# Laying out the transposed Q/K buffer by head: one buffer and one scratch format of a gated attention and feed-forward kernel

## The chip, the core and the metric

The kernel runs on one core of one Trainium2 chip. The metric is the device time of one execution in microseconds (us), as the median over several executions. The profile comes from one further execution, whose own time is given beside its span.

## What is computed

Two branches run over the same 2048 rows of 1024 values and are mixed by a sigmoid gate. Branch B is a feed-forward net of width 3584. Branch A is attention with a recurrent memory: the rows are cut into 64 segments of 32, each segment sees 8 memory rows ahead of it, and the first 8 rows of its output are the memory of the next segment. So the segments of branch A run strictly one after the other.

```python
def _A_ref(x, mem0, Wq, Wk, Wv, Wo, seg_len):       # 32 heads of 128, M = 8, seg_len = 32
    mem = mem0
    for s in range(n_seg):                          # 64 segments
        xs = x[:, s * seg_len:(s + 1) * seg_len, :].copy()
        h = jnp.concatenate([mem, xs], axis=1)      # 40 rows
        q = jnp.einsum('btd,dhe->bhte', h, Wq)
        k = jnp.einsum('btd,dhe->bhte', h, Wk)
        v = jnp.einsum('btd,dhe->bhte', h, Wv)
        scores = jnp.einsum('bhqe,bhke->bhqk', q, k) * scale
        scores = jnp.where(mask[None, None], scores, -1000000000.0)
        p = _softmax(scores, axis=-1)
        o = jnp.einsum('bhqk,bhke->bhqe', p, v)
        o = jnp.einsum('bhte,hed->btd', o, Wo)
        mem = o[:, :M, :].copy()
        outs.append(o[:, M:, :])
...
g = _sigmoid((x * gate_w).sum(-1, keepdims=True))
return g * a + (1 - g) * b                          # b = (gelu(x @ w_gate) * (x @ w_up)) @ w_down
```

All inputs and weights are bf16.

## The kernel before

**Stages.** Branch B comes first (to about 600 us of the span). Then the 64 segments of branch A follow, some 24.8 us each. The weights of branch A do not all fit on the chip: most lie in the buffers `arena`, `low`, `extra` and so on; 14 pieces of 512 KB per segment are read again each time into `ring`, a ring of 8 slots of which one piece takes two. SyncE's queue issues such a load (line 693) when the matmuls that used the slots before are done, so that up to four are under way.

**Rows of a segment.** A segment's 40 rows are split. Its 8 memory rows and the last 24 of its own rows (together 32, in `hT`) are projected when the segment runs (`emit_P`, line 1087). The first 8 rows of every segment ("ext" rows in the code) do not depend on the memory; they are projected earlier for four segments at once (`emit_ext`, line 897, 4 x 8 rows in `xe`), in rounds that a hand-written list puts between the other matmuls (token `F`). When such a projection is complete, `end_rows` takes it from the bank `pbc` to `rowsx`. For Q and K it is then transposed (`go`, line 1010), taken from PSUM back into the same `rowsx` by four VectorE copies, one for each of the four segments (`put`, line 1023), and written by a GpSimd DMA to the DRAM scratch `qk_scr` (line 1026). `load_ext` reads a segment's part of it into `pn` one segment ahead (line 795).

**Q and K of a segment.** The work is done in two halves `h` of 16 heads. A projection puts its 32 rows four times beside each other: partitions 32g to 32g+31 of a bank hold the rows for the four heads i = 0..3 of group g. The bank goes to `rows`, and `emit_T` (matmuls of line 1133, copy of line 920 or 922) transposes it, so that a PSUM bank holds, for each of the 128 dimensions of a head, values in the order (i, g, row). The copy moves these to the buffer `qk`, and `emit_qke` (line 1152 on ScalarE for the half 0, line 1154 on VectorE for the half 1) puts the 8 ext rows of each head behind them. In each segment `emit_T` runs four times, with its copy twice on VectorE and twice on ScalarE.

**Scores.** `emit_S` (line 1171) then forms the 40 x 40 scores of 16 heads with 16 matmuls. Two heads run beside each other, one with its result on partitions 0 to 39, one on 64 to 103; each has its own Q as stationary operand (40 columns) and its own K as moving operand (40 columns). The softmax follows (VectorE lines 1178 to 1189, ScalarE's exponential in line 1184, VectorE line 1194), then its transposition (`emit_PT`, line 1204), the product with V (`emit_PV`, line 1231) and the output projection (`emit_O`, line 1279). At the end of a segment `mem` and `mem_T` (line 1345, copies in lines 1352 and 1355) bring the new memory into `hT`.

**The order.** Nothing reorders at run time. `PLAN` is a list of tokens by hand, the same for all segments but the first, that says in which order the operations are put into the engines' queues; every engine runs its own in that order and waits on semaphores. `F` carries four numbers, one for each place of a segment in a group of four: so many waiting rounds of the ext projections or the ext rows' output are put there. These pieces of it matter here:

```python
("T", 1, "dve", 32, 4), ("P", "q", 1, 2), ("F", (1, 1, 0, 0)), ("P", "q", 1, 2), ("F", (10, 0, 0, 6)), ("flush", 128, 4),
("S", 0), ("P", "k", 1, 2), ...
("PV", 0, 4, "act", "act"), ("S", 1), ("F", (1, 1, 5, 0)), ("O", 0, 2), ...
("M", 1, "act"), ("MT", 1), ("F", (0, 1, 1, 0)), ("OB", 1), ("bh", 0, "act"), ("M", 0, "dve"), ("F", (0, 0, 1, 1)), ("flush", 128, 3)
```

`flush` is `go` and `put` of a finished ext projection. `put_out` (line 1358, VectorE) comes early in the next segment: it reads a finished segment's output from its bank `pba` or `pbb`, which the projections of the next segment use again.

Between its uses for scores `qk` also holds a piece of a weight (`flat_qk`, written as flat memory by line 1067 and read by lines 1087 and 897).

Of the kernel before, what the change touches and what calls it, by code (L numbers as in the profile page):

```python
# [5 lines left out]
BF16 = mybir.dt.bfloat16  # L6
# [122 lines left out]
def bass_gated_mix__memory_aug_recurrent_mem_tr__geglu_ffn__prompt_kernel(  # L129
# [21 lines left out]
    SEG = 32  # L151
    L = SEG + M
# [11 lines left out]
    EXT = 8  # L164
    GR = 4
    QK_RES, V_RES, O_RES = 6, 6, 4

    with ExitStack() as es:
# [23 lines left out]
        def SB(shape, dt, name):  # L192
            return es.enter_context(nc.sbuf_tensor(name, list(shape), dt))
# [3 lines left out]
        xe = nc.alloc_sbuf_tensor_at("xe", [128, KC, SEG], BF16, offset=LOW + 14336)  # L197
        rows = SB([128, 512], BF16, "rows")
        rowsx = SB([128, 512], BF16, "rowsx")
        qk = SB([128, 2, 4, L, 4], BF16, "qk")  # L200
        vt = SB([128, 2, 512], BF16, "vt")
        pn = SB([128, 8, 80], BF16, "pn")
        pnf = pn[:, :, :].rearrange("p a b -> p (a b)")
# [1 line left out]
        qkst = [pnf[:, 256 * h:256 * (h + 1)] for h in range(2)]  # L205
# [20 lines left out]
        PBV = [p[:, :].bitcast(BF16) for p in PB]  # L226
# [4 lines left out]
        g = _Sched()  # L231
# [16 lines left out]
        def A(c):  # L248
# [6 lines left out]
           r=[("ident",)], w=[("ident",)])  # L255
# [67 lines left out]
        for side in range(2):  # L323
            op("pool", lambda e, side=side: e.memset(bm[64 * side:64 * side + L, side:side + 1], 1.0),
               r=[("bm",)], w=[("bm",)])
# [312 lines left out]
        for tok, *arg in PLAN:  # L638
            if tok in ("P", "O", "OA"):
# [3 lines left out]
                for x in range(x0, x0 + n):  # L643
                    k = KORD[who][x] if tok == "P" else OORD[who[1]][x]
                    u = (*who, k - k % 2 if tok != "P" and (*who, k) not in wide else k)
# [272 lines left out]
        def copy(eng, dst, src, r, w):  # L918
            if eng == "act":
                op("act", lambda e: e.activation(dst, src, ACTF.Copy), r=r, w=w)  # L920
            else:
                op("dve", lambda e: e.tensor_copy(dst, src), r=r, w=w)
# [48 lines left out]
        for s in range(NSEG):  # L971
# [18 lines left out]
            def end_rows(m, h, j):  # L990
                if s == 0:
                    rx, kx, sx = stage(m, h)
                else:
                    flush()
                    rx, kx, sx = rowsx[:, :], RX, "rowsx"
                op("act", lambda e: e.activation(rx, PB[B_X][:, :], ACTF.Copy), r=[P(B_X)], w=kx)  # L996
                if m == "v":
                    def put():
                        op("pool", lambda e: e.dma_start(v_scr[j, h, :, :, :, :].rearrange("g u r c -> (g u r) c"), rx),
                           r=kx, w=[("vscr", j, h)], dsem="%sv" % sx)  # L1000
                    vput.append(put) if s == 0 else put()
                    return
                mi = "qk".index(m)

                def go(w=32, bank=B_T):
                    def mk(e):
                        ins = None
                        for i in range(4):
                            for y in range(0, 128, w):
                                ins = e.transpose(PBV[bank][y:y + w, i * 128:(i + 1) * 128],  # L1010
                                                  rx[:, i * 128 + y:i * 128 + y + w], ident[:, :])
                        return ins
                    op("pe", mk, r=[*kx, ("ident",)], w=[P(bank)])
                    return bank

                def put(bank):
                    st = rx.rearrange("p (u g r i) -> p u g r i", u=GR, g=4, r=EXT)
                    src = PBV[bank][:, 0:512].rearrange("p (i g u r) -> p u g r i", i=4, g=4, u=GR)

                    def cp(e):  # L1020
                        ins = None
                        for u in range(GR):
                            ins = e.tensor_copy(st[:, u], src[:, u])
                        return ins
                    op("dve", cp, r=[P(bank)], w=kx)
                    op("pool", lambda e: e.dma_start(  # L1026
                        qk_scr[j * GR:(j + 1) * GR, :, h, mi, :].rearrange("u p x -> p u x"),
                        rx.rearrange("p (u x) -> p u x", u=GR)),
                       r=kx, w=[("qkscr", j, h, mi)], dsem=sx)
                post.append((go, put))  # L1030


# [95 lines left out]
            def emit_T(m, eng="dve", w=32, bank=B_T):  # L1128
                def mk(e):
                    ins = None  # L1130
                    for i in range(4):
                        for j in range(0, 128, w):
                            ins = e.transpose(PBV[bank][j:j + w, i * 128:(i + 1) * 128],  # L1133
                                              rows[:, i * 128 + j:i * 128 + j + w], ident[:, :])
                    return ins
                op("pe", mk, r=[("rows",), ("ident",)], w=[P(bank)])
                copy(eng, qk[:, m, :, 0:SEG, :], PBV[bank][:, 0:512].rearrange("p (i g c) -> p g c i", i=4, g=4),
                     [P(bank)], [("qk", m)])

            def emit_qke(h, eng="dve", s=s, ms=(0, 1)):  # L1140
                if s == 0:
                    for mi in ms:
                        m = "qk"[mi]
                        rx, kx, _ = stage(m, h)
                        src = rx[:, 0:128].rearrange("p (g x) -> p g x", g=4)
                        op("dve", lambda e, mi=mi, src=src: e.tensor_copy(
                            qk[:, mi, :, SEG:L, :].rearrange("p g c i -> p g (c i)"), src), r=kx, w=[("qke",)])
                    return
                dst = qk[:, :, :, SEG:L, :].rearrange("p m g c i -> p m g (c i)")
                src = qkst[h].rearrange("p (m g x) -> p m g x", m=2, g=4)  # L1150
                if eng == "act":
                    op("act", lambda e: e.activation(dst, src, ACTF.Copy), r=[("qkst", h)], w=[("qke",)])
                else:
                    op("dve", lambda e: e.tensor_copy(dst, src), r=[("qkst", h)], w=[("qke",)])
# [9 lines left out]
            def emit_S(h, s=s):  # L1164
                def mk(e):
                    ins = None
                    for x in range(8):
                        for side in range(2):
                            p0 = SIDES[side]
                            gq = 2 * (x // 4) + side  # L1170
                            ins = e.matmul(PB[B_S][p0:p0 + L, x * L:(x + 1) * L],  # L1171
                                           lhsT=qk[:, 0, gq, :, x % 4], rhs=qk[:, 1, gq, :, x % 4], start=True, stop=True,
                                           skip_group_check=True)
                    return ins
                op("pe", mk, r=[("qk", 0), ("qk", 1), ("qke",)], w=[P(B_S)])
                sv = PB[B_S][0:104, 0:8 * L].rearrange("p (i c) -> p i c", i=8)
                mxv = mx[0:104, :]
                op("dve", lambda e: e.scalar_tensor_tensor(  # L1178
                    out=sv, in0=sv, scalar=scale, in1=mask[0:104, None, :].to_broadcast([104, 8, L]),
                    op0=ALU.mult, op1=ALU.add), r=[("mask",)], w=[P(B_S)])  # L1180
                op("dve", lambda e: e.tensor_reduce(mxv, sv, AX.X, ALU.max), r=[P(B_S)], w=[("mx",)])
                op("dve", lambda e: e.tensor_tensor(out=sv, in0=sv, in1=mxv[:, :, None].to_broadcast([104, 8, L]),  # L1182
                                                    op=ALU.subtract), r=[("mx",)], w=[P(B_S)])
                op("act", lambda e: e.activation(sv, sv, ACTF.Exp), w=[P(B_S)])  # L1184
                if s and h == 0:
                    emit_qke(1)
                op("dve", lambda e: e.tensor_reduce(mxv, sv, AX.X, ALU.add), r=[P(B_S)], w=[("mx",)])  # L1187
                op("dve", lambda e: e.reciprocal(mxv, mxv), w=[("mx",)])
                op("dve", lambda e: e.tensor_tensor(  # L1189
                    out=rr[0:104, :, :], in0=mx[0:104, :, None].to_broadcast([104, 8, 2]),  # L1190
                    in1=bm[0:104, None, :].to_broadcast([104, 8, 2]), op=ALU.mult), r=[("mx",), ("bm",)], w=[("rr",)])
                gates = [("z", t) for t in range(NT)] + [("th", t) for t in range(NT)] if s == 0 and h == 0 else []
                for c0, k0, n in ((0, 0, SEG), (2 * SEG, SEG, EXT)):
                    op("dve", lambda e, c0=c0, k0=k0, n=n: e.tensor_tensor(  # L1194
                        out=pn[0:104, :, c0:c0 + 2 * n].rearrange("p i (two c) -> p i two c", two=2),
                        in0=sv[:, :, None, k0:k0 + n].to_broadcast([104, 8, 2, n]),
                        in1=rr[0:104, :, :, None].to_broadcast([104, 8, 2, n]), op=ALU.mult),
                       r=[P(B_S), ("rr",)], w=[("pn", c0), ("qkst", 0), ("qkst", 1)] + PTB + gates)
# [363 lines left out]
```

## Time and profile before

| | |
|---|---|
| device time, median of 3 executions | 2206.41 us (2202.46 to 2207.2) |
| the profiled execution: device time | 2207.77 us |
| the profiled execution: span from the first to the last instruction | 2205.9 us |
| mean granted TensorE clock in it | 0.994 |
| VectorE, ScalarE, GpSimd busy | 52%, 42%, 21% of the span |
| read from and written to HBM | 596.71 MB and 34.59 MB |

In the profile PE is TensorE's matmuls, PEld its loads of the stationary operand (they overlap matmuls), DVE is VectorE, ACT ScalarE, POOL GpSimd and SP SyncE; a q behind an engine's name is its DMA queue. A group of the profile is written as line, engine, operation, output and input; the banks of PSUM are `pba` to `pbh`. A matmul's recorded duration is the time until its last result stands, most of which is the way through the array; matmuls that follow each other overlap, so what a block of them costs is seen from start to start.

### The profile page before, as it was taken

The page shows a single profiled execution, that of the slowest core. Times are in us where ns is not written, and L with a number is a line of the kernel's source. Part 1 is how long each engine was busy: PE and PEld are TensorE (multiplying, and loading weights), DVE is VectorE, ACT ScalarE, POOL GpSimd, SP SyncE. Part 2 cuts the span into 40 slices and gives each one's busy share as a digit, 9 for nine tenths or more (in the row PEclk, how much of TensorE's full clock was granted, in tenths as well). Part 3 has the DMA queues.
Part 4 walks back from the last instruction along what each step waited for, and adds up shares of the span by engine and source line. Part 5 has one row for each costly group of instructions (what it writes and reads, how often), then busy time and mean ns, then how long its engine had stood idle before and what let it go on. Part 6 is the DMA issues. An engine that isn't in the chain of part 4 may idle for free.

```text
span 2205.9 us, 78545 instructions
## 1 busy us (share of the span) xinstructions
PE 2104.6 (95%) x35368; PEld 1107.8 (50%) x35424; DVE 1154.8 (52%) x2680; ACT 935.6 (42%) x1960; POOL 461.6 (21%) x814
## 2 busy tenths in 40 slices
PE   9999999999998999999999999999999999999987
PEld 4444444444454555555454545555455555555544
DVE  5716536345054555555555555555555555555554
ACT  4403324133044444544454445444444444444443
POOL 1020020140122222222122222222122222222221
PEclk9999999999999999999999999999999999999999
DMA  8726625346888999999999999999999999999997
GB/s 271 276 70 220 215 58 194 122 148 202 302 302 301 325 326 328 326 338 328 330 317 327 325 319 329 323 324 320 315 323 328 332 330 329 337 333 323 324 325 245
DMA packets 247377, 629.21 MB, mean 285 GB/s; under 512 B 37393, under 2 KB 106081, under 8 KB 246273
## 3 DMA queue, kind: packets, MB, share of 16 engines
q1 hardware_dynamic: 215732, 573.14, 74.5%
q0 software_dynamic: 30112, 50.48, 7.4%
q8 instruction: 278, 4.55, 0.8%
q10 hardware_dynamic: 1196, 0.56, 0.1%
q14 instruction: 59, 0.48, 0.1%
HBM read 596.71 MB, written 34.59 MB: 286 GB/s over the span
## 4 chain that ended last, share of the span: by engine, by line
PE 77%; DMA 15%; DVE 4%; ACT 2%; issue 2%; POOL 0%; SPq 0%; DVEq 0%; POOLq 0%; ACTq 0%
PE pba L1087 13%; PE pbb L1087 12%; DMA ring<-w_scr 11%; PE pbc L897 6%; PE pbb L1279 4%; DMA hT<-xT_scr 3%; PE pba L1279 3%; PE pbc L1258 3%; PE pba L466 2%; PE pbh L466 2%; PE pbg L466 2%; PE pbf L466 2%; PE pbe L466 2%; PE pbb L466 2%; PE pbd L466 2%; PE pbc L466 2%
## 5 line engine op out<-in xcount | busy, mean ns | idle before, releaser
L1087 PE MATMUL pba<-arena,hT 128*32 128x512 bf16 x4416 | 357.1, 383 | 5.1 <-DVE bo L1358 4.4
L1087 PE MATMUL pbb<-arena,hT 128*32 128x512 bf16 x4416 | 355.6, 383 | 1.3 <-issue 1.3
L897 PE MATMUL pbc<-arena,xe 128*32 128x512 bf16 x2208 | 190.0, 381 | 3.4 <-ACT rowsx L996 2.0
L803 POOL DMA_DIRECT2D vt<-v_scr x252 | 140.7, 561 | 146.8 <-PE pba L1087 94.3
L1087 PEld LDWEIGHTS pba<-arena,hT 128*32 128x32 bf16 x4416 | 109.2, 97 | 112.1 <-ACT rows L1074 11.0
L1087 PEld LDWEIGHTS pbb<-arena,hT 128*32 128x32 bf16 x4416 | 113.4, 97 | 99.2 <-DVE hT L1355 6.2
L1087 PE MATMUL pba<-ring,hT 128*32 128x512 bf16 x1286 | 127.2, 384 | 18.5 <-DMA ring<-w_scr 16.7
L1184 ACT ACTIVATE pbd<-pbd 104x320 f32<-104x320 f32 x128 | 53.0, 414 | 215.3 <-DVE pbd L1182 215.3
L1087 PE MATMUL pbb<-ring,hT 128*32 128x512 bf16 x1280 | 126.4, 384 | 7.8 <-DMA ring<-w_scr 7.2
L920 ACT ACTIVATE rows<-pba 128x512 bf16<-128x512 f32 (+1 forms) x130 | 67.1, 516 | 150.2 <-PE pba L1087 126.0
L1194 DVE TENSOR_TENSOR pn<-pbd,rr 104x512 bf16<-104x512 f32 (+1 forms) x256 | 125.7, 491 | 9.3 <-DVE rr L1189 0.6
L920 ACT ACTIVATE rows<-pbb 128x512 bf16<-128x512 f32 x127 | 66.0, 520 | 149.5 <-PE pbb L1087 119.5
L1026 POOL DMA_DIRECT2D qk_scr<-rowsx x60 | 47.5, 792 | 365.2 <-DVE pbd L1178 171.5
L1178 DVE SCALAR_TENSOR_TENSOR pbd<-pbd,mask 104x320 f32<-104x320 f32 x128 | 63.5, 496 | 102.0 <-PE pbd L1171 102.0
L1279 PE MATMUL pbb<-arena,oT 128*32 128x256 bf16 (+1 forms) x2304 | 115.8, 268 | 0.0
L1279 PE MATMUL pba<-arena,oT 128*32 128x256 bf16 (+1 forms) x2320 | 112.7, 269 | 0.1
L477 ACT ACTIVATE arena<-arena 128x512 f32<-128x512 f32 x112 | 70.5, 629 | 97.6 <-DVE arena L474 97.6
L821 POOL DMA_DIRECT2D bo<-b_scr x63 | 35.6, 565 | 341.8 <-PE pba L1087 235.9
L920 ACT ACTIVATE oT<-pbe 128x256 bf16<-128x256 f32 x192 | 73.6, 384 | 48.7 <-PE pbe L1231 47.4
L920 ACT ACTIVATE qk<-pbe 128x512 bf16<-128x512 bf16 x127 | 75.5, 594 | 36.4 <-PE pbe L1133 35.1
L1187 DVE TENSOR_REDUCE mx<-pbd 104x8 f32<-104x320 f32 x128 | 62.9, 491 | 53.5 <-ACT pbd L1184 53.5
L1133 PEld LDWEIGHTS pbe<-ident,rows 128*32 128x32 bf16 (+1 forms) x1560 | 46.0, 96 | 77.6 <-ACT rows L920 50.4
(308 smaller groups left out, 4519.5 us busy)
## 6 DMA issues: line engine op xcount, KB each, us to landing
ring<-w_scr SPq DMA_DIRECT2D x896, 512.0 KB, 5.5
arena<-in_B_w_gate_dram SPq DMA_DIRECT2D x27, 1024.0 KB, 5.4
arena<-in_B_w_up_dram SPq DMA_DIRECT2D x27, 1024.0 KB, 8.3
pn<-qk_scr POOLq DMA_DIRECT2D x63, 128.0 KB, 5.3
qk_scr<-rowsx POOLq DMA_DIRECT2D x60, 128.0 KB, 5.0
arena<-in_B_w_down_dram SPq DMA_DIRECT2D x7, 1024.0 KB, 11.4
arena<-in_A_Wk_dram SPq DMA_DIRECT2D x6, 1024.0 KB, 6.9
arena<-in_A_Wv_dram SPq DMA_DIRECT2D x6, 1024.0 KB, 10.1
```

The source lines that it names most:

```text
L466: ins = e.matmul(PB[bank][:, :], lhsT=wv[:, kc, col:col + 128], rhs=xb[:, kc, :], start=(kc == 0), stop=(kc == KC - 1))
L477: op("act", lambda e: e.activation(tp[q], tp[q], ACTF.Tanh, scale=C_GELU), r=[("tp", q)] + mr, w=[("tp", q)])
L803: op("pool", lambda e, side=side: e.dma_start(vt[p0 + side * EXT:p0 + (side + 1) * EXT, :, :], v_scr[s // GR, h, side::2, s % GR, :, :].re ...
L897: ins = e.matmul(PB[B_X][32 * gq:32 * gq + 32, :], lhsT=xe[:, us[-1], :], rhs=us[gq // 2][0][gq % 2], start=(n == 0), stop=(n == KC - 1), ...
L920: op("act", lambda e: e.activation(dst, src, ACTF.Copy), r=r, w=w)
L1087: ins = e.matmul(PB[bank][32 * gq:32 * gq + 32, :], lhsT=hT[:, kc, :], rhs=us[gq // 2][0][gq % 2], start=(x == 0), stop=(x == KC - 1), ski ...
L1178: op("dve", lambda e: e.scalar_tensor_tensor(out=sv, in0=sv, scalar=scale, in1=mask[0:104, None, :].to_broadcast([104, 8, L]), op0=ALU.mul ...
L1184: op("act", lambda e: e.activation(sv, sv, ACTF.Exp), w=[P(B_S)])
L1187: op("dve", lambda e: e.tensor_reduce(mxv, sv, AX.X, ALU.add), r=[P(B_S)], w=[("mx",)])
L1194: op("dve", lambda e, c0=c0, k0=k0, n=n: e.tensor_tensor(out=pn[0:104, :, c0:c0 + 2 * n].rearrange("p i (two c) -> p i two c", two=2), in0 ...
L1258: ins = e.matmul(PB[B_X][b:b + 32, :], lhsT=oe[:, o * 8 + k, :], rhs=u[c], start=(n == 0), stop=(n == H - 2), skip_group_check=True)
L1279: ins = e.matmul(PB[B_O][32 * q:32 * q + 32, c0:c1], lhsT=oT[:, o % 2, k, :], rhs=u[q // 2][:, (q % 2) * 256 + c0:(q % 2) * 256 + c1], sta ...
```

## The change

Two layouts change together; which instructions are issued, on which engine and in which order, stays as it was.

- `qk` held, for each dimension, (Q or K, group, position, head of the group): at each of the 40 positions the four heads of a group stood side by side, so the 40 values of one head were 4 elements (8 bytes) apart. Now it holds (group, head, Q or K, position): the 40 values of a head's Q are adjacent, its 40 K values follow, 80 elements per head. It has 1280 elements as before.
- The ext rows' format in `rowsx`, `qk_scr` and `pn` was (segment, group, row, head) and is (segment, group, head, row).

The copies and the matmuls address the new places:

```diff
-        qk = SB([128, 2, 4, L, 4], BF16, "qk")
+        qk = SB([128, 4, 4, 2, L], BF16, "qk")
...
                 def put(bank):
-                    st = rx.rearrange("p (u g r i) -> p u g r i", u=GR, g=4, r=EXT)
-                    src = PBV[bank][:, 0:512].rearrange("p (i g u r) -> p u g r i", i=4, g=4, u=GR)
+                    st = rx.rearrange("p (u g i r) -> p u g i r", u=GR, g=4, r=EXT)
+                    src = PBV[bank][:, 0:512].rearrange("p (i g u r) -> p u g i r", i=4, g=4, u=GR)
...
-                copy(eng, qk[:, m, :, 0:SEG, :], PBV[bank][:, 0:512].rearrange("p (i g c) -> p g c i", i=4, g=4),
+                copy(eng, qk[:, :, :, m, 0:SEG], PBV[bank][:, 0:512].rearrange("p (i g c) -> p g i c", i=4, g=4),
...
-                        src = rx[:, 0:128].rearrange("p (g x) -> p g x", g=4)
+                        src = rx[:, 0:128].rearrange("p (a r) -> p a r", a=16)
                         op("dve", lambda e, mi=mi, src=src: e.tensor_copy(
-                            qk[:, mi, :, SEG:L, :].rearrange("p g c i -> p g (c i)"), src), r=kx, w=[("qke",)])
+                            qk[:, :, :, mi, SEG:L].rearrange("p g i r -> p (g i) r"), src), r=kx, w=[("qke",)])
                     return
-                dst = qk[:, :, :, SEG:L, :].rearrange("p m g c i -> p m g (c i)")
-                src = qkst[h].rearrange("p (m g x) -> p m g x", m=2, g=4)
+                dst = qk[:, :, :, :, SEG:L].rearrange("p g i m r -> p m (g i) r")
+                src = qkst[h].rearrange("p (m a r) -> p m a r", m=2, a=16)
...
-                                           lhsT=qk[:, 0, gq, :, x % 4], rhs=qk[:, 1, gq, :, x % 4], start=True, stop=True,
+                                           lhsT=qk[:, gq, x % 4, 0, :], rhs=qk[:, gq, x % 4, 1, :], start=True, stop=True,
```

What each access looks like before and after, in runs of adjacent elements per partition:

| access | before | after |
|---|---|---|
| `emit_T`, read from PSUM | single elements, 128 elements apart | 16 runs of 32 |
| `emit_T`, write to `qk` | 4 runs of 128 | 16 runs of 32 |
| `put`, read from PSUM (each of 4 copies) | single elements, 128 elements apart | 16 runs of 8 |
| `put`, write to `rowsx` | one run of 128 | one run of 128 |
| `emit_qke`, read from `pn` | one run of 256 | one run of 256 |
| `emit_qke`, write to `qk` | 8 runs of 32 | 32 runs of 8 |
| `emit_S`, stationary and moving operand | single elements, 4 elements apart | one run of 40 each |

## The prediction

> **What bounds the kernel now.** First the page: its busy times and its chain of work that ended last.
>
> ```profile
> PE 2104.6 (95%) x35368; PEld 1107.8 (50%) x35424; DVE 1154.8 (52%) x2680; ACT 935.6 (42%) x1960; POOL 461.6 (21%) x814
> ...
> PE 77%; DMA 15%; DVE 4%; ACT 2%; issue 2%; POOL 0%; SPq 0%; DVEq 0%; POOLq 0%; ACTq 0%
> ```
>
> TensorE is busy nearly always and holds 77% of the chain; the rest is mostly DMA. Both layouts are used only by the attention stage, so I read that next: two groups of four segments from the view by windows, and the longest waits of TensorE's matmuls.
>
> ```profile
> 1292.79:1390.20 97.41, 93.56 (x2034) 51.73 (x2030) 54.70 (x142) 47.66 (x99) 23.97 (x41) 1.00 0.95 327
> 1390.20:1490.11 99.91, 93.87 (x2032) 51.96 (x2028) 54.60 (x142) 47.78 (x99) 23.99 (x41) 1.00 0.92 321
> ```
>
> ```profile
> PE pba L1087 <- DMA ring<-w_scr: 16.7, 26, 1.9
> PE pbd L1231 <- DVE pn L922: 10.6, 32, 0.4
> PE pbe L1345 <- ACT rows L920: 9.7, 33, 0.4
> PE pbb L1087 <- DMA ring<-w_scr: 7.2, 15, 1.4
> PE pbb L1087 <- DVE hT L1352: 6.1, 10, 1.7
> PE pba L1087 <- DVE bo L1358: 4.4, 14, 0.6
> ```
>
> Columns of the first: window, its length, busy time of PE, PEld, DVE, ACT, POOL, granted clock, DMA share, GB/s. Four segments take 97 to 100 us with 93.6 to 93.9 us of it on PE, while VectorE has over 40 us free. The DMA engines are at 0.92 to 0.95, so the weight stream is the second limit: it is kept going by the matmuls that free ring slots, and it is late often enough to cost 24 us (second view, 16.7 + 7.2). Time is won here by taking work or waits from PE's own queue, and the ring may hand some of it back.
>
> **The scores' matmuls, the main term.** One block of `emit_S`, with what follows it, from the timeline of PE; then its group and three others for comparison, by tile (ns as min/median/max).
>
> ```profile
> 1242.87 0.50 PE L1171 MATMUL pbd<-qk 128*40 128x40 bf16 x16
> 1243.29 0.40 PE L1087 MATMUL pba<-ring,hT 128*32 128x512 bf16 x4
> ...
> 80.30 0.35 PE L421 MATMUL pbh<-ident,oe 8*128 8x8 bf16 x8
> ```
>
> ```profile
> L1171 PEld LDWEIGHTS pbd<-qk x2048: 113/130/138, 614.4 to 2187.6; 128*40 128x40 bf16 x187
> L1171 PE MATMUL pbd<-qk x2048: 196/197/218, 614.4 to 2187.7; 128*40 128x40 bf16 x187
> ...
> L1204 PEld LDWEIGHTS pbe<-ident,pn x1024: 112/117/117, 622.1 to 2192.5; 104*80 104x80 bf16 x171
> ...
> L1087 PEld LDWEIGHTS pbb<-qk,hT x64: 92/93/102, 637.3 to 2172.7; 128*32 128x32 bf16 x64
> L1087 PE MATMUL pbb<-qk,hT x64: 379/389/609, 637.5 to 2172.7; 128*32 128x512 bf16 x64
> ...
> L421 PE MATMUL pbh<-ident,oe x8: 161/161/175, 80.3 to 80.5; 8*128 8x8 bf16 x8
> ```
>
> Does the 8-byte step cost TensorE anything? Both operands say so. A load of 32 adjacent columns takes 92 ns at the least, of 80 adjacent ones 112, that is 0.42 ns per column; 40 adjacent ones should take 95, the strided 40 take 113. A matmul over 8 columns takes 161 ns and over 512 takes 379, 0.43 ns per column; 40 should take 175 and take 197. Both are over by some 20 ns, about as much as 40 columns cost at all: the strided operands go at half speed. The two loads of a pair go to different columns of the array, and at half speed one after the other they would need 67 ns. The pairs are closer than that: 0.50 - 0.20 us is 0.30 from the first start to the last, seven steps between the eight pairs, 43 ns each. So the loads overlap, and stream plus hand-over set the step.
>
> With adjacent columns the stream of a pair falls to 17 ns. The step can't fall as far: eight matmuls of 8 columns one after another still take (0.35 - 0.16) / 7 = 27 ns each. I take 27 as the new step: 7 x 16 ns = 0.11 us per block. Its bounds are 0 (the step is set by something else) and 0.16 (the whole 23 ns per step that half-speed streaming makes up, 43 to 20). There are 128 blocks: 14.1 us.
>
> A rule of the Trainium skill speaks against this term: "Advanced Engine Details and Errata", section "SBUF Cachelines", says that reads which hit the same 16-byte line run at full speed, and that two hits on a line are enough. Steps of 8 bytes make two hits, so by that rule the old layout is at full speed and the term is 0; 113 ns against 95 says otherwise here.
>
> Not every block is on the path. In the last segment of each group of four, and in the last four, no ext round stands between the second block and the output projection, which waits for ScalarE:
>
> ```profile
> 1199.50 0.39 ACT L920 ACTIVATE oT<-pbe 128x256 bf16<-128x256 f32 x1 [0.36 <-PE pbe L1231]
> ...
> 1199.40 0.50 PE L1171 MATMUL pbd<-qk 128*40 128x40 bf16 x16
> 1199.94 0.29 PE L1279 MATMUL pbb<-low,oT 128*32 128x256 bf16 x4
> ```
>
> The copy ends at 1199.89 and the projection starts at 1199.94: the block hides in that wait and a shorter one gains nothing. That is 16 + 3 = 19 blocks by the list. 109 x 0.11 = 12.0 us remain.
>
> **The copies out of PSUM.** Groups from the view by tile and by line:
>
> ```profile
> L922 DVE COPY qk<-pbe x65: 690/692/693, 607.7 to 2177.8; 128x512 bf16<-128x512 bf16 x65
> ...
> L1067 DVE COPY qk<-pbh x62: 678/680/682, 660.4 to 2170.5; 128x1024 bf16<-128x1024 bf16 x62
> ...
> L1023 DVE COPY rowsx<-pbd x120: 277/280/292, 689.8 to 2073.9; 128x128 bf16<-128x128 bf16 x120
> ...
> L922 DVE COPY pn<-pbe 80x320 bf16<-80x320 bf16 x128 | 41.0, 321 | 13.3 <-PE pbe L1204 9.2
> L922 DVE COPY rows<-pbe 80x480 bf16<-80x480 bf16 x64 | 25.7, 402 | 69.8 <-PE pbe L1204 69.8
> ```
>
> VectorE takes 692 ns for 512 elements read one by one and 680 for 1024 adjacent ones. Runs of 40 go at the fast rate: (402 - 321) / 160 = 0.51 ns per element, so 512 elements in runs of 32 should take 402 + 32 x 0.51 = 418 ns, 274 less. What waits for these copies? The scores matmuls follow several projection quads later: no wait of L1171 for them is among the long ones above. I cost the gain at nothing; its cover is those quads. `put`'s four copies should fall by 128 x (1.04 - 0.52) = 67 ns each, if runs of 8 are as good as runs of 40; else by nothing. They start one after the other, so a set is 0.27 us shorter.
>
> One set matters. At the end of some segments VectorE runs it ahead of `put_out`, and a projection waits for that to get its bank:
>
> ```profile
> 1185.32 0.87 DVE L1023 COPY rowsx<-pbd 128x128 bf16<-128x128 bf16 x4
> 1186.11 0.48 DVE L1358 SCALAR_TENSOR_TENSOR bo<-pba,pbd,bo 128x256 bf16<-128x256 f32 x1
> ```
>
> This wait is 4.4 us in 14 times (above), 0.31 each; 0.27 less in most of them is 3.5 us (0 to 4.4). What is late next there is the transposed memory of L1345, which waits for ScalarE, unchanged.
>
> ScalarE shows no price for single elements or for short runs, so its copies stay:
>
> ```profile
> L920 ACT ACTIVATE qk<-pbe x127: 591/597/599, 616.8 to 2185.1; 128x512 bf16<-128x512 bf16 x127
> L1152 ACT ACTIVATE qk<-pn x63: 408/417/418, 640.2 to 2174.7; 128x256 bf16<-128x256 bf16 x63
> L1154 DVE COPY qk<-pn x63: 215/216/218, 648.4 to 2180.8; 128x256 bf16<-128x256 bf16 x63
> ...
> L1074 ACT ACTIVATE rows<-pbf 128x512 bf16<-128x512 bf16 x63 | 37.6, 597 | 43.1 <-PE pbe L1345 42.8
> L920 ACT ACTIVATE oe<-pbe 128x64 bf16<-128x64 f32 x129 | 28.7, 223 | 0.0
> ...
> DVE mx L1187 <- ACT pbd L1184: 53.5, 128, 0.5
> ```
>
> 597 ns with single elements equals 597 with adjacent ones (L1074), and `oe`'s 64 elements in runs of 8 take 223, on the same line (597 - 448 x 0.83 = 225). The one copy that could lose is L1154, which now writes runs of 8 where it wrote 32. At its fast rate it stays at 216 ns; at one element per step it would take 692 - 256 x 1.04 = 426. It stands behind the exponential's start, where VectorE waits 53.5 / 128 = 0.42 us anyway: 0.21 more is covered; without that cover it would be 63 x 0.21 = 13 us. I take nothing. The DMAs of L1026 and L795 move the same bytes in the same shape.
>
> **What the ring gives back.** Late loads, from the waits for line 693, beside all its loads:
>
> ```profile
> L693 SPq DMA_DIRECT2D ring<-w_scr x896: 319/320/2516, 507.0 to 2189.2; - x180
> ...
>   PEld pba L1087: 36.8, 65
>   PEld pbb L1087: 25.9, 56
> ```
>
> 121 of 896 loads, 14%, were waited for. Four are under way at any time; when one of them is late, what PE saves between its issue and its use is waited away. Independent, one in four late would be 1 - 0.86^4 = 45%; late ones come in strings, so I take a third.
>
> **The sum.** (12.0 + 3.5) x 2/3 = 10.3 us off the profiled execution's 2207.8 gives 2197.5. That execution was 1.4 above the median of the three; counted from the median it is 2196.1. I forecast 2197. Its own range: with steps of 20 ns and a quarter given back (109 x 0.16 + 4.4) x 3/4 = 16 us (2190), with half of the step's gain and half given back (6.0 + 3.5) / 2 = 5 us (2202).
>
> **The rivals.**
> 1. *The step stays (no gain).* Its price was the pair's two weight loads, 2 x 17 ns one after the other, plus hand-over, and the 113 ns only latency. The 43 ns would fit as well. Against it: the matmuls are 20 ns too long too, and four loads of 92 ns in L1087 show no queueing. Only L1358's 3.5 x 2/3 = 2.3 us remain: 2205.
> 2. *The ring takes all.* DMA at 0.93 is the true pace, and each saved ns is waited for at the next load. For it: the DMA share; against it: 86% of the loads are in time. Near 2206.
> 3. *Slower: an earlier scratch store.* `put` ends sooner, so the 60 stores of L1026 (128 KB each) start earlier and fall among ring loads at another place. A late load costs PE 23.9 / 41 = 0.6 us on average. If each store made one more load late, 36 us would be lost against 10.3 gained; from 18 of 60 on the kernel is slower. At 30 of 60 it comes to 2206 + 8 = 2214. For it: POOL's queue is 21% busy and its waits set when these start; against it: four times 67 ns is a small shift.
> 4. *More than forecast.* Steps of 20 ns and nothing given back, 109 x 0.16 + 4.4 = 22 us: 2185.
>
> **How the numbers follow.** Forecast 0.53, rival 1 0.12, rival 2 0.08, rival 3 0.17, rival 4 0.10. About 0.2%, 4.4 us, is what a measurement can tell from no change. Faster: 0.53 x 0.94 + 0.10 + some of rival 1 = 0.62; slower: 0.17; same: 0.21. The range from 2186 to 2208 leaves out half of rival 4 and most of rival 3. The likeliest's own range, 2190 to 2202, lies below no change.
>
> **What would show it.** A block of L1171 taking 0.39 us instead of 0.50, its loads 95 ns at the least and matmuls about 176: the main term. Still 0.50: rival 1. L922 into `qk` near 418, L1023 near 213 and L1358's wait under 1 us: the copies; L1023 at 280 or L1154 near 426 would show that runs of 8 lose the fast rate. ScalarE's 597 and 417 unchanged. Waits for the ring grown from 24 us to about 29: a third given back; to 40: rival 2; with waits of L1026's neighbours up and the time above 2211: rival 3. A step that falls while the time does not would mean that PE isn't what sets the end.

## The result, and the profile after

| | before | after |
|---|---|---|
| median of 15 executions each, same chips | 2207.23 us (2201.6 to 2214.05) | 2194.7 us (2181.08 to 2204.84) |
| ratio of the times | | 0.9944, 95% interval 0.9925 to 0.9963 |
| the profiled execution: device time, span | 2207.77, 2205.9 us | 2194.3, 2192.5 us |

The change saves 12.5 us, 0.56%; the forecast was 2197 against 2206.41. The page of the changed kernel, its busy times and its chain of work:

```profile
PE 2082.4 (95%) x35368; PEld 1084.1 (49%) x35424; DVE 1104.2 (50%) x2680; ACT 935.1 (43%) x1960; POOL 460.9 (21%) x814
...
PE 75%; DMA 18%; DVE 3%; ACT 2%; issue 1%; POOL 0%; SPq 0%; DVEq 0%; ACTq 0%
```

PE is 22 us less busy and VectorE 51 us; ScalarE is where it was. The chain holds less of PE and more of DMA. The groups on `qk` and `put`'s copies, by tile (ns as min/median/max):

```profile
L1171 PEld LDWEIGHTS pbd<-qk x2048: 95/97/100, 616.2 to 2173.8; 128*40 128x40 bf16 x187
L1171 PE MATMUL pbd<-qk x2048: 178/179/198, 616.2 to 2173.8; 128*40 128x40 bf16 x187
L920 ACT ACTIVATE qk<-pbe x127: 591/592/598, 618.5 to 2171.1; 128x512 bf16<-128x512 bf16 x127
L922 DVE COPY qk<-pbe x65: 423/424/426, 609.7 to 2166.0; 128x512 bf16<-128x512 bf16 x65
...
L1152 ACT ACTIVATE qk<-pn x63: 407/417/418, 645.7 to 2162.9; 128x256 bf16<-128x256 bf16 x63
L1154 DVE COPY qk<-pn x63: 215/215/218, 653.6 to 2168.7; 128x256 bf16<-128x256 bf16 x63
...
L1023 DVE COPY rowsx<-pbe x120: 211/214/226, 651.6 to 2047.7; 128x128 bf16<-128x128 bf16 x120
```

The loads of the scores' stationary operand fell from 113 ns at the least to 95, the matmuls from 197 to 179. VectorE's copies fell from 692 to 424 and from 280 to 214 ns, and 129 x 0.268 + 256 x 0.066 makes up the 51 us. L1154, which now writes runs of 8, kept its 215 ns, and ScalarE's copies did not move.

What this did to the order of PE and VectorE shows at the place where a segment's first scores block stands behind a flush. First the kernel before, then the changed one, from the timelines of PE and of VectorE:

```profile
1242.54 0.40 PE L1010 MATMUL pbe<-ident,rowsx 128*128 128x128 bf16 x4
...
1244.00 0.38 PE L1133 MATMUL pbe<-ident,rows 128*128 128x128 bf16 x4
...
1242.97 0.88 DVE L1023 COPY rowsx<-pbe 128x128 bf16<-128x128 bf16 x4 [0.70 <-PE pbe L1010]
```

```profile
1046.09 0.40 PE L1010 MATMUL pbe<-ident,rowsx 128*128 128x128 bf16 x4
1046.42 0.38 PE L1171 MATMUL pbd<-qk 128*40 128x40 bf16 x16
1046.72 0.40 PE L1087 MATMUL pba<-ring,hT 128*32 128x512 bf16 x4
1046.95 0.39 PE L1087 MATMUL pba<-arena,hT 128*32 128x512 bf16 x4
1047.28 0.39 PE L1133 MATMUL pbe<-ident,rows 128*128 128x128 bf16 x4
...
1046.52 0.61 DVE L1023 COPY rowsx<-pbe 128x128 bf16<-128x128 bf16 x4 [0.97 <-PE pbe L1010]
```

The block takes 0.38 us instead of 0.50, and the next matmul starts 0.30 us after its first in place of 0.42: 0.12 per block. But look at the transposition L1133 that follows: `emit_T` needs the bank `pbe`, which `put` is still reading. It starts 0.15 us after `put`'s last copy ends in both kernels (1243.85 to 1244.00, 1047.13 to 1047.28). From L1010 to L1133 it is 1.46 us before and 1.19 after, and the 0.27 between them is `put`'s. Over all 30 places of this kind the medians are 1.46 and 1.20 us. Here the shorter scores block alone would have gained nothing (e10 below shows it). This wait is not in the prediction.

Both kernels issue the same 35368 matmuls, in the same order but for 27 places, so the time from the start of one to the start of the next can be compared one by one. The steps into the scores blocks of all segments but the first add up to 23.1 us before and 22.9 after. The steps into the transpositions L1010 of these segments, which write a bank that `emit_T`'s copy may still be reading, add up to 14.7 and 15.4. So PE's queue did not feel that VectorE's copies into `qk` became 0.27 us shorter.

The waits of PE's matmuls in the changed kernel:

```profile
PE pba L1087 <- DMA ring<-w_scr: 19.5, 30, 1.5
PE pbb L1087 <- DMA ring<-w_scr: 16.4, 23, 2.0
...
PE pbb L1279 <- ACT oT L920: 2.9, 17, 0.2
```

Waits for the ring rose from 23.9 to 35.9 us, each in one profiled execution. L1358's wait, 4.4 us before, is gone from the list. And a new one has come: the output projection's for ScalarE, 17 times here and twice more into `pba`, behind the 19 blocks that the prediction had taken out as hidden.

### The profile page after: what moved, and what is told of

It reads as the page before. It is cut to its first block, busy times and chain, and to the rows that moved or that the text cites. A ratio compares the mean times of both kernels' runs of the same rounds, so it can differ in the third digit from the quotient of the medians.

```text
span 2192.5 us, 78545 instructions
## 1 busy us (share of the span) xinstructions
PE 2082.4 (95%) x35368; PEld 1084.1 (49%) x35424; DVE 1104.2 (50%) x2680; ACT 935.1 (43%) x1960; POOL 460.9 (21%) x814
## 4 chain that ended last, share of the span: by engine, by line
PE 75%; DMA 18%; DVE 3%; ACT 2%; issue 1%; POOL 0%; SPq 0%; DVEq 0%; ACTq 0%
DMA ring<-w_scr 13%; PE pba L1087 13%; PE pbb L1087 12%; PE pbc L897 7%; PE pbb L1279 5%; PE pba L1279 3%; DMA hT<-xT_scr 3%; PE pbc L1258 3%; PE pbg L466 2%; PE pbh L466 2%; PE pbf L466 2%; PE pbe L466 2%; PE pba L466 2%; PE pbe L1204 2%; PE pbe L1231 2%; PE pbb L466 2%
## 5 line engine op out<-in xcount | busy, mean ns | idle before, releaser
L1087 PE MATMUL pba<-ring,hT 128*32 128x512 bf16 x1286 | 127.4, 384 | 21.8 <-DMA ring<-w_scr 19.5
L1279 PE MATMUL pbb<-arena,oT 128*32 128x256 bf16 (+1 forms) x2304 | 115.4, 267 | 0.2 <-issue 0.2
L1279 PE MATMUL pba<-arena,oT 128*32 128x256 bf16 (+1 forms) x2320 | 112.0, 267 | 0.0
L1133 PEld LDWEIGHTS pbe<-ident,rows 128*32 128x32 bf16 (+1 forms) x1560 | 45.6, 96 | 74.1 <-ACT rows L920 65.7
```

Of the source, the lines that this page charges most:

```text
L1087: ins = e.matmul(PB[bank][32 * gq:32 * gq + 32, :], lhsT=hT[:, kc, :], rhs=us[gq // 2][0][gq % 2], start=(x == 0), stop=(x == KC - 1), ski ...
L1279: ins = e.matmul(PB[B_O][32 * q:32 * q + 32, c0:c1], lhsT=oT[:, o % 2, k, :], rhs=u[q // 2][:, (q % 2) * 256 + c0:(q % 2) * 256 + c1], sta ...
```

## The experiments

| | what it undoes or changes | median, us | the kernel before beside it | ratio (95%) |
|---|---|---|---|---|
| e1 | `put` one element at a time, both ways | 2288.88 | 2203.1 | 1.0406 (1.0373 to 1.0438) |
| e2 | `emit_T`'s copies one element at a time, both ways | 2506.98 | 2203.1 | 1.1367 (1.1335 to 1.1399) |
| e3 | scores' operands 8 bytes apart, `emit_T`'s copies as before, fast `put` | 2200.35 | 2203.1 | 0.9995 (0.9973 to 1.0016) |
| e10 | adjacent operands, `put` as before | 2200.51 | 2205.91 | 0.9981 (0.9963 to 0.9999) |
| e11 | changed kernel, `emit_qke` in two copies | 2196.19 | 2205.91 | 0.9953 (0.9935 to 0.9971) |
| e7 | kernel before, half of the ring's bytes | 2148.38 | 2205.35 | 0.9747 (0.9722 to 0.9772) |
| e8 | changed kernel, half of the ring's bytes | 2126.87 | 2205.35 | 0.9651 (0.9627 to 0.9675) |
| e12 | one step of `PLAN` moved | 2200.11 | 2205.91 | 0.9973 (0.9954 to 0.9992) |
| e4, e5, e6, e9 | steps of the scores' operands | 2196.19, 2206.77, 2199.33, 2601.14, one execution each | | |

The ratio comes from the single executions of both kernels and is not exactly the quotient of the two medians: in e3 it is 0.9995, and the quotient 0.9988.

**e1: `put` as slow as before, as it was meant.**

```diff
-                    st = rx.rearrange("p (u g i r) -> p u g i r", u=GR, g=4, r=EXT)
-                    src = PBV[bank][:, 0:512].rearrange("p (i g u r) -> p u g i r", i=4, g=4, u=GR)
+                    st = rx.rearrange("p (u g i r) -> p u g r i", u=GR, g=4, r=EXT)
+                    src = PBV[bank][:, 0:512].rearrange("p (i g u r) -> p u g r i", i=4, g=4, u=GR)
```

> The changed kernel, but the four copies of put read and write one element at a time (L1023), as before the change; all layouts stay. My theory: the faster put is worth two waits, the one of a projection for L1358 (4.4 us before, 0.0 after) and one of the transposition L1133 behind a flush (7.4 us less after), so with L1023 at 280 ns again both waits come back and the time is 5 to 9 us above the changed kernel: about 0.997 to 0.998 of the kernel before. Rival, that the scores' matmuls alone make the gain: 0.994, as the changed kernel.

It came out at 1.04, far outside both. The layouts stayed, so to read one by one it also had to write one by one, 16 bytes apart, and that was new. Its copies by line:

```profile
L1023 DVE COPY rowsx<-pbd x120: 719/928/970, 698.2 to 2154.3; 128x128 bf16<-128x128 bf16 x120
```

A set of them from VectorE's timeline, and then the longest waits of PE:

```profile
760.98 2.40 DVE L1023 COPY rowsx<-pbe 128x128 bf16<-128x128 bf16 x4 [0.97 <-PE pbe L1010]
```

```profile
PE pbe L1133 <- DVE rowsx L1023: 50.3, 30, 1.7
PE pba L1087 <- DVE bo L1358: 25.3, 15, 1.7
```

A copy takes 928 ns and not 280. As a test of the 280 it failed; as a magnifying glass it served: a `put` that is 1.79 us longer (2.40 against 0.61) makes L1133 wait 1.7 us in exactly 30 segments. So the changed kernel has hardly any slack there, and L1358 is the second that waits.

**e2: `emit_T`'s copies as slow as before, as it was meant.**

```diff
-                copy(eng, qk[:, :, :, m, 0:SEG], PBV[bank][:, 0:512].rearrange("p (i g c) -> p g i c", i=4, g=4),
+                copy(eng, qk[:, :, :, m, 0:SEG].rearrange("p g i c -> p g c i"), PBV[bank][:, 0:512].rearrange("p (i g c) -> p g c i", i=4, g=4),
```

> The changed kernel, but emit_T's copies into qk go one element at a time again (VectorE 692 ns); all layouts stay. My theory: these copies are covered by the projections that stand between them and the scores, so the time stays that of the changed kernel, 0.993 to 0.996 of the kernel before. Rival, that the 0.27 us per copy was on the path: with two VectorE copies per segment up to 126 x 0.27 x 2/3 = 23 us lost, a ratio of 0.998 or more.

The same failure, larger. By tile:

```profile
L920 ACT ACTIVATE qk<-pbe x127: 2305/2373/2496, 620.7 to 2488.0; 128x512 bf16<-128x512 bf16 x127
...
L922 DVE COPY qk<-pbd x64: 2371/2408/2455, 625.3 to 2477.7; 128x512 bf16<-128x512 bf16 x64
```

Writing 512 single elements 160 bytes apart takes 2.4 us on either engine. Whether the 0.27 us that VectorE's copies into `qk` gained is worth anything was therefore not settled by this run. A test without scattered writes needs the old layout, and there the scores' operands are stepped too. What settles it are the steps into the scores blocks and into L1010, compared above: they did not get shorter.

**e10 and e11: `put` as slow as before, without scattered writes.** e10 keeps the new `qk` but puts the old format into `rowsx` and `qk_scr`, so that `put` reads singly and writes one run, as before the change; the sorting moves to `emit_qke`'s read, in two copies. e11 has those two copies and the new format. Against the changed kernel, e10 has among others:

```diff
-                    st = rx.rearrange("p (u g i r) -> p u g i r", u=GR, g=4, r=EXT)
-                    src = PBV[bank][:, 0:512].rearrange("p (i g u r) -> p u g i r", i=4, g=4, u=GR)
+                    st = rx.rearrange("p (u g r i) -> p u g r i", u=GR, g=4, r=EXT)
+                    src = PBV[bank][:, 0:512].rearrange("p (i g u r) -> p u g r i", i=4, g=4, u=GR)
...
+            return [(qk[:, :, :, mi, SEG:L], part.rearrange("p (g r i) -> p g i r", g=4, r=EXT))]
```

> The new qk buffer with the old format of rowsx and qk_scr: put reads one element at a time and writes one run (L1023 at 280 ns, as before the change, without the scattered writes of e1), emit_qke sorts the ext rows while it reads, in two copies. My theory, that put is late for the transposition behind the first scores block and for L1358: both waits are back (4 us each, and the 3.5 us of the shorter first blocks that are swallowed by the first), 6 to 9 us above the next run, about 0.997 to 0.999 of the kernel before. Rival, that only the scores' matmuls matter: as the next run.

> The changed kernel with emit_qke's copy cut in two, as in e3 and e10: what the second copy alone costs. My theory: covered by the exponential, 0.994 to 0.996. If the second copy is on the path of the scores: 0.997 or more, and e3 and e10 overstate what they undo.

e11 lies within the interval of the changed kernel. e10 is 0.0028 above it, 6.2 us at 2206 (4.3 between the medians), as expected; the two intervals overlap by 0.0008, so the size is rough. The profile of e10 has its own line numbers (L1142 is `emit_T`, L1032 `put`, L1368 `put_out`). By tile, `put`'s copies:

```profile
L1032 DVE COPY rowsx<-pbe x120: 278/281/293, 650.0 to 2057.8; 128x128 bf16<-128x128 bf16 x120
```

And among the waits of PE the two that were expected:

```profile
PE pbe L1142 <- DVE rowsx L1032: 6.1, 28, 0.2
...
PE pba L1096 <- DVE bo L1368: 4.2, 14, 0.3
```

The first was not on the list of the kernel before, because the longer scores block filled most of it: PE stood idle there for 0.09 us, in e10 for 0.21. Over the 30 places, the median from L1010 to L1133 is 1.465 us in e10 and 1.464 in the kernel before, 1.305 in e3 (the old scores block with the fast `put`) and 1.197 in the changed kernel. So here the shorter block alone gains nothing, the faster `put` alone 0.16 us, and both together 0.27.

**e3: the scores' operands back at 8 bytes.** Q and K each in the old order (group, position, head), the new `put`, and `emit_qke` in two copies. With the old order `emit_T`'s copies read single elements again too.

```diff
+                return part.rearrange("p (g c i) -> p g i c", g=4, c=L)
```

> The qk buffer as before the change (both operands of the scores 8 bytes apart), with the new format of rowsx and qk_scr, so that put stays fast. My theory: a block of L1171 is back at 0.50 us, its loads at 113 ns, its matmuls at 196; L1023 stays at 214 ns; the time is 7 to 10 us above the changed kernel, 0.997 to 0.999 of the kernel before. Rival, that the copies make the gain: 0.994 with the block at 0.50.

By tile:

```profile
L1196 PE MATMUL pbd<-qk x2048: 196/197/217, 617.3 to 2185.7; 128*40 128x40 bf16 x187
```

```profile
L1165 DVE COPY qk<-pbe x65: 691/692/694, 610.8 to 2177.7; 128x512 bf16<-128x512 bf16 x65
```

Measured 0.9995: 0.0042 above e11, which has the same two copies, 9 us by the ratios (4.2 between the medians, from different chips, so the size is rough). The intervals of the two (e3 from 0.9973, e11 up to 0.9971) just separate. A block is back at 0.50 us, L1023's counterpart stays at 215 ns and L1358's wait stays gone. The time lies just above what was expected, and that is within its interval. By itself e3 brings back two things, the stepped operands and the 692 ns of VectorE's copies into `qk`. But the steps into its scores blocks (23.1 us) and into the transpositions (14.7) are those of e11 within 0.2 us, so these copies have no visible part in the loss.

**e4, e5, e6, e9: which operand, which step.** Each ran once, to show its blocks; its copies into `qk` differ, so its time is not compared. e4 has K 8 bytes apart and Q adjacent, e5 the reverse; e6 has both 4 bytes apart (two heads side by side), e9 both 16 bytes apart (eight).

```diff
+            return qkf[:, 640 * mi:640 * (mi + 1)].rearrange("p (g j c b) -> p g j b c", g=4, j=2, b=2)
...
+            return qkf[:, 640 * mi:640 * (mi + 1)].rearrange("p (y c k i) -> p y k i c", y=2, k=2, i=4)
```

> Q adjacent as after the change, K 8 bytes apart as before; two copies in emit_qke in place of one. My theory, that the moving operand's stream sets the step of the pairs: a block of L1171 takes 0.48 to 0.50 us, matmuls 196 ns, loads 95 to 97. Rival, that the loads of the stationary operand set it: 0.38 to 0.39 us.

> K adjacent, Q 8 bytes apart. My theory: loads of 113 ns or more, but a block of 0.38 to 0.41 us, since loads overlap the matmuls. Rival, that the loads set the step: 0.48 to 0.50 us.

> Both operands of the scores 4 bytes apart (two heads side by side); emit_T's and emit_qke's copies are two in place of one. If a stepped operand goes at half speed whatever the step: loads of 113 ns, matmuls of 196, a block of 0.50 us. If the speed goes by the bytes passed over, as much of a row per cycle as two adjacent elements or more: 97, 179 and 0.38 us, as when adjacent.

> Both operands 16 bytes apart (eight heads side by side); copies in two. If a stepped operand goes at half speed whatever the step: 113 ns, 196 ns and 0.50 us. If the speed goes by the bytes passed over: a quarter of the speed, loads near 150 ns, matmuls near 230, pairs 73 ns apart and a block near 0.75 us.

In all four the first fence is one block from PE's timeline, the second the loads and matmuls by tile (the line of the scores' matmuls is L1196 or L1188 there). e4, K stepped:

```profile
848.93 0.47 PE L1196 MATMUL pbd<-qk 128*40 128x40 bf16 x16
```

```profile
L1196 PEld LDWEIGHTS pbd<-qk x2048: 95/110/114, 613.5 to 2176.1; 128*40 128x40 bf16 x187
L1196 PE MATMUL pbd<-qk x2048: 195/209/214, 613.5 to 2176.1; 128*40 128x40 bf16 x187
```

e5, Q stepped:

```profile
852.25 0.50 PE L1196 MATMUL pbd<-qk 128*40 128x40 bf16 x16
```

```profile
L1196 PEld LDWEIGHTS pbd<-qk x2048: 112/130/138, 613.4 to 2186.4; 128*40 128x40 bf16 x187
L1196 PE MATMUL pbd<-qk x2048: 179/194/228, 613.4 to 2186.4; 128*40 128x40 bf16 x187
```

e6, both 4 bytes apart:

```profile
847.31 0.38 PE L1188 MATMUL pbd<-qk 128*40 128x40 bf16 x16
```

```profile
L1188 PEld LDWEIGHTS pbd<-qk x2048: 95/97/102, 613.5 to 2179.2; 128*40 128x40 bf16 x187
```

e9, both 16 bytes apart:

```profile
904.29 0.83 PE L1188 MATMUL pbd<-qk 128*40 128x40 bf16 x16
```

```profile
L1188 PEld LDWEIGHTS pbd<-qk x2048: 149/172/181, 615.9 to 2580.7; 128*40 128x40 bf16 x187
L1188 PE MATMUL pbd<-qk x2048: 252/258/291, 615.9 to 2580.7; 128*40 128x40 bf16 x187
```

Taking a matmul's own duration off a block and dividing by the seven steps: 37 ns per pair with K stepped, 44 with Q stepped, 43 with both (the kernel before), 28 with none. So for Q and K the theory had it the wrong way round: a stepped stationary operand alone (e5, its rival's 0.50 us) brings back the whole old step, a stepped moving operand alone (e4, 0.47 us, below the 0.48 to 0.50 expected) somewhat over half of the difference. The two do not add; it looks as if the slower one set the step. e6 shows that a step of 4 bytes costs nothing. In e9 the step is 82 ns, nearly twice that of 8 bytes, and the block of 0.83 us and the matmuls of 258 ns are above the 0.75 and 230 expected. The excess of the shortest load over 95 ns is 0, 18 and 54 ns for 4, 8 and 16 bytes, that is 0, 1 and 3 times 18. For the loads it looks as if a column of 4 bytes came for free and every further 4 bytes passed over cost as much as one more column. The matmuls fit less well: the shortest of them exceed the changed kernel's 178 ns by 18 and 74 ns for 8 and 16 bytes.

**e7 and e8: both kernels without the ring's waits.** From its 33rd load on, each load of the ring brings half of its elements; the other half of the weights is left out.

```diff
-            op("sp", lambda e: e.dma_start(ring[:, sl:sl + wd, :].rearrange("p a b -> p (a b)"), src),
+            part = wd * (1024 if n_str[0] <= 32 else 512)
+            op("sp", lambda e: e.dma_start(ring[:, sl:sl + wd, :].rearrange("p a b -> p (a b)")[:, 0:part], src[:, 0:part]),
```

> The kernel before, in which each load of the ring after the first 32 brings only the first half of its elements; the other half is left out and keeps what lay there, so the output is not the reference's. My theory: the waits for the ring fall from 24 us to under 8 and the time falls by some 20 to 30 us. Only its distance to the next run matters.

> The changed kernel with the same loads left out. My theory, that the ring gives back a good third of what TensorE saves: without ring waits the two kernels lie 18 to 24 us apart, against 12.5 with them. Rival, that the ring gives nothing back: 12 to 13 us apart.

e7 fell by 57 us where 20 to 30 were expected, more than the waits for the ring alone (24 us); what else the lighter stream gave was not followed. The two lie 21.5 us apart, as expected (0.0096 in the ratio, each known to 0.0025). e8's only waits for the ring are these:

```profile
PE pbb L1280 <- DMA ring<-w_scr: 0.6, 1, 0.6
...
PE pba L1088 <- DMA ring<-w_scr: 0.2, 1, 0.2
```

With a stream that is hardly ever late the change is worth 21.5 us. The traces of the two show where, by the steps of PE's matmuls one by one: 9.8 us at 79 scores blocks, 8.0 at the 30 places behind `put` (scores block and wait together), 4.0 at L1358's 15 waits and 0.0 at the 19 hidden blocks, 21.8 in all. With the real stream the change saves 12.5 us at the medians, so the ring hands back 9 us, 42%. But by the interval of that ratio the saving is 8 to 17 us, and what is handed back between a quarter and six tenths. Whether earlier scratch stores (rival 3's mechanism) have a part in it, no run separates.

**e12: filling the wait behind the second scores block.**

```diff
-("S", 1), ("F", (1, 1, 5, 0)), ("O", 0, 2), ("F", (0, 0, 2, 1)), ("PV", 1, 4, "act", "act"), ("F", (0, 0, 0, 1)), ("P", "v", 1, 1), ("O", 0, 1)
+("S", 1), ("F", (1, 1, 5, 0)), ("P", "v", 1, 1), ("O", 0, 2), ("F", (0, 0, 2, 1)), ("PV", 1, 4, "act", "act"), ("F", (0, 0, 0, 1)), ("O", 0, 1)
```

> The changed kernel with one step of PLAN moved: the third round of P v 1 stands behind the second scores block, ahead of the first two rounds of the output projection, in place of behind PV 1. My theory: in the 19 segments where the projection waits for ScalarE behind a bare scores block, 0.22 us of that wait is filled, 4 us in all, of which the ring takes a part: 0.992 to 0.994. Rival, that the moved round meets a late ring load there, or that PV 1 and what follows it gets later: 0.995 or more.

0.9973: no gain over the changed kernel, as the rival had it. (The moved round is the fourth of `P v 1` in the list.) The new wait of L1279 for ScalarE is gone, and the waits for the ring are the longest again:

```profile
PE pba L1087 <- DMA ring<-w_scr: 27.7, 39, 3.5
...
PE pbb L1087 <- DMA ring<-w_scr: 10.4, 18, 1.5
```

They are 38.1 us against 35.9 in the changed kernel and 32.9 in e11, each in one execution. What took the expected gain was not settled. No version ran faster than the changed kernel with the whole computation.

## Why the prediction was right, and where it was not

- **PE's queue is what counts, with the ring behind it.** Right. Work off PE's queue came through, and the ring took part of it.
- **The scores' matmuls.** The block went to 0.38 us (0.39 forecast), the loads to 95 ns (95), the matmuls to 179 (176), the step to 28 ns (27). That operands stepped by 8 bytes go at half speed was right. What was wrong is the reason given for the step: "the loads overlap, and stream plus hand-over set the step". e5 shows that stepped loads alone hold the pairs 44 ns apart. The forecast came out because both operands became adjacent together. Making K alone adjacent, which is e5, leaves the block at 0.50 us, where the prediction's reason would have promised most of the gain.
- **The rule about cachelines.** By the rule that the prediction takes from the Trainium skill, "Advanced Engine Details and Errata", section "SBUF Cachelines", two hits per 16-byte line would have left the old layout at full speed. The runs disagree for TensorE: its shortest loads take 95, 113 and 149 ns at 4, 8 and 16 bytes.
- **The 19 hidden blocks.** Right: there the projection's wait for ScalarE has appeared, 17 + 2 times by the list.
- **The copies.** 424 ns (418 forecast) and 214 (213), L1154 unchanged (unchanged). L1358's wait fell by 4.4 us (3.5). The copies into `qk` were costed at nothing, and PE's steps into their readers bear it out: they did not get shorter.
- **The missed wait.** "One set matters" was wrong: two do. In 30 segments the transposition behind the first scores block waits for `put`. From L1010 to L1133 it gained 30 x 0.27 = 8.1 us. Of this the prediction had booked 30 x 0.11 = 3.3 under the scores blocks, where it would not have come without the faster `put`.
- **What the ring gives back.** A third was forecast; 42% was measured at the medians (9 of 21.5 us), anything from a quarter to six tenths by the interval. So the third is neither confirmed nor refuted. The waits for the ring grew to 35.9 us, between the 29 that were named for a third and the 40 named for everything.
- **The sum, by what was measured.** In PE's queue the change is worth 9.8 + 8.0 + 4.0 = 21.8 us (e7 and e8, step by step), and 21.5 between their medians. The forecast had 15.5: the missed wait is most of the difference. The ring took 9 of it, where a third would have been 7. The larger gain and the larger give-back partly offset each other, so that 10.3 came as near to 12.5 as it did is in part luck; the direction and the main term are not.
- **The rivals.** Rival 1 is out (the step fell), though e5 shows that the loads, which it named, do weigh on the step. Rival 2 is out as a whole, since the time fell by 12.5 us, though its mechanism took the rest. Rival 3, slower by earlier stores, did not come true, since the time fell; whether a part of it hides in what the ring took was not tested. Rival 4's step of 20 ns was not reached.

## What to carry to other kernels

Read a small operand's layout from the engine that reads it most: here both operands of 2048 small matmuls stood 8 bytes apart, and the profile told it before the change, by loads and matmuls some 20 ns longer than their columns cost elsewhere. When work is taken from the limiting engine, look for what is late next at the very place, here an in-order copy that still holds a PSUM bank: in 30 of 128 blocks the shorter matmuls were worth nothing without the faster copy. And where a weight stream keeps the DMA engines busy for 0.93 of the time, book only part of each saving: here about 58% stayed, a figure known only roughly.

## What the runs showed of the hardware that was not expected

- **Scattered writes of 2-byte elements are dear on both VectorE and ScalarE; scattered reads from PSUM cost VectorE a factor of two and ScalarE nothing.** Reading single elements 256 bytes apart and writing runs, VectorE took 692 ns for 512 elements and in runs 424, that is 1.04 and 0.52 ns for each element besides a fixed 159 ns; ScalarE took 597 and 592. Writing them singly 160 bytes apart, VectorE took 2408 (e2: (2408 - 159) / 512 = 4.4 ns each), and ScalarE went from 592 to 2373 ((2373 - 171) / 512 = 4.3 ns each, 171 being its fixed part at 0.83 ns per element). At 16 bytes it is 5 to 6 ns on VectorE (e9: (1432 - 159) / 256 = 5.0; e1: (928 - 147) / 128 = 6.1, with the 147 ns that remain of `put`'s 214 at 0.52 each). At 4 bytes it is 1.1 ns each, twice the price of runs: in e6 256 elements took 442 ns, (442 - 159) / 256.

The same 256 elements written 4 bytes apart (first, e6) and 16 bytes apart (second, e9), from the views by tile, 442 against 1432 ns:

```profile
L1157 DVE COPY qk<-pbd x128: 423/442/457, 619.3 to 2170.3; 128x256 bf16<-128x256 bf16 x128
```

```profile
L1157 DVE COPY qk<-pbd x128: 1303/1432/1569, 624.1 to 2565.3; 128x256 bf16<-128x256 bf16 x128
```

- **Runs of 8 keep the fast rates**: 214 ns for 128 elements from PSUM, 215 for 256 from SBUF, as with runs of 32 and 40.
- **TensorE's operands cost by the bytes passed over**: 4 bytes per element are free, 8 cost about double and 16 about fourfold (the shortest loads of 40 columns take 95, 113 and 149 ns, of which the 40 columns make up 17 when adjacent). The load of the stationary operand weighs more on the step than the moving stream: 44 ns against 37 when only one of them is stepped.
